# Weight copies from doubled loads, a split rounding step, the last odd skip on VectorE, and a new instruction order

## The chip, the cores and the metric

The kernel runs on one core of one Trainium2 chip. The metric is the device time of one execution in microseconds. A run of the profiler gives one execution in detail, with a time of its own. All times below are microseconds unless marked otherwise.

## The reference

Two independent branches read two inputs of 2048 positions by 448 features, and their results stand side by side in the output.

```python
# branch A: 16 heads of 28, each position looks at itself and 7 earlier ones, 2 apart
qkv = x @ wqkv                              # 448 -> 3 * 448
idx = pos[:, None] - arange(8)[None] * 2    # masked where negative
logits = einsum("bhsd,bhswd->bhsw", q, kg) * 28 ** -0.5
o = einsum("bhsw,bhswd->bhsd", softmax(logits), vg) @ wo
# branch B: a diagonal complex recurrence over 2048 steps
Bu = einsum("bld,pd->blp", x, B_bar)        # B_bar from Lambda, dt, B
h = Lam_bar * h + Bu[:, t]                  # for every t
y = 2 * einsum("blp,dp->bld", hseq, C).real + x * Dskip
```

Tensors are bf16 in memory.

## The kernel before

**Layout.** Positions are paired: even and odd positions become two "parities", so that the window with step 2 is contiguous within a parity. `xA` and `xB` hold the two inputs transposed, 7 chunks of 128 rows by 1024 position pairs. Since 448 is three and a half times 128, the fourth chunk holds 64 rows of each parity, and matmuls over 448 features run as pairs of half-height (64-row) matmuls, one for each parity, side by side in the array. Each pair writes its own half of a two-bank PSUM unit; there are four such units (pool `mm`, function `unit`). A weight therefore must lie in both halves of the partitions. A pair's 14 matmuls are split into a part of 8 (node name with a trailing underscore) and a part of 6; between the two a one-element GpSimd memset, a "tick", keeps the halves in order (`pair`, `relay`, `halves`).

**Branch A.** Nodes v0 to v7 compute V for 128 pairs each, nodes q{1 or 0}{s}{c} compute K (1) or Q (0) for head group s and column chunk c (256, 256 and 512 columns); ev and eq nodes copy the results out of PSUM, on ScalarE or VectorE. V's weights `Wv` are loaded once, and VectorE copies them to the other partition halves (vw0 to vw2). The first two blocks of `xA` come as rows and are transposed on TensorE (xt0, xt1, copied out by xe00 to xe11); the other six come through transposing DMAs. The weights of Q and K are loaded once into `Wraw`, four chunks high, and copied into `Wpad`, in which each head's 28 columns are padded to 32 and both halves are filled. That copy is the node wp{q}{z} (`n_wp`, for Q or K and for half z of the heads): five instructions, since rows move across partition halves. Attention goes over 9 blocks: node s{parity}{b} computes a block's scores with quarter-height (32-row) matmuls, first a mask (line 740), then the heads (line 744); x nodes take the exponential on ScalarE; a{b} multiplies by V with full-height matmuls of 29 columns; n{b} normalizes on VectorE; ot{b} transposes the result by a DMA; vi{b} builds the shifted window of V by DMAs. Nodes w0 to w7 multiply by `wo` and we nodes copy the result out.

**Branch B.** Small vectors are loaded into `rows` and turned by node tr; pA, pB, e1, e2, p2, p3a and p3b work out constants. A table of sines and cosines over 512 steps is made by t0 (ScalarE), tk and ts (VectorE), t2 (sine), t3 (a sign bit cleared, 2048 elements a partition) and t4 (cosine). l1 and l2 scale the B matrices, wtx transposes them by DMA into `WT`; b{half}{k} multiplies x by them (98 512-column matmuls in all, line 804), be evacuates; ma, ri, sc, mb and ro turn, scan and turn back on VectorE, 7 state chunks in two halves of 512 steps. ctn and ctl load and transpose C, cg and ch nodes form two scaled copies `C1` and `C2`; g0 and g1 form a product for the even positions. y{t} gives the even rows of an output block and z{t} the odd rows. The odd rows also need x times Dskip: for blocks 0 to 3 by four small diagonal matmuls in z{t}, for blocks 4, 5 and 6 (`YD`) on VectorE, which forms the products ahead (xd{t}) and adds them while it copies z{t} out (ye{t}1). Block 7 is cut into columns 0 to 319 (z70, ye71) and 320 to 447 (z71, ye72), with its diagonal matmuls, so that the last store is small.

**Order.** The program is a list of nodes, each with costs for the engines that may run it, what it depends on, a rank, and for some an earliest time (`at`). Class `Plan` simulates the engines with those numbers, takes the ready node of the lowest rank whenever an engine is free, and so fixes the order in each engine's queue; the queues then run in that order and wait only for data. A rank is a line in an index for each kind of node (`RANK`). A change of tile shape on TensorE is priced by `TURN`, 0.1 us. Loads are written first, in a fixed order, most of them on SP's queue; each load that is issued by SP or ScalarE uses one of eight semaphores in turn, so an issue also waits until the load eight before it has landed. Two of the small vectors go by GpSimd's own queue.

Of the kernel before, what the change touches and what calls it, by code (L numbers as in the profile page):

```python
# [7 lines left out]
BF16 = mybir.dt.bfloat16  # L8
F32 = mybir.dt.float32
I32 = mybir.dt.int32  # L10
# [16 lines left out]
RANK = {"vi": (-544.75, 131.055), "v": (-110.39, 34.569), "q0": (63.48, 25.419), "q1": (-1326.93, 228.142), "s": (-380.99, 73.488), "a": (-188.15, 159.093),  # L27
        "b0": (56.3, -31.172), "b1": (2986.12, -242.123), "d0": (94.79, 241.448), "d1": (1628.45, -108.947), "l": (2486.1, 164.979), "t": (251.37, -53.356),
        "tk": (731.53, 100.376), "xd": (2178.91, -29.053), "cg": (593.37, 8.672), "ch": (1143.63, -50.034), "g": (436.44, 143.698), "y": (468.94, 183.089),
        "w": (1186.02, 1.256), "gu": (1304.36, -293.628), "q2": (430.19, -21.545), "wp": (-27.3, 132.469)}  # L30


class Plan:


    WAKE, TURN = 0.13, 0.1
# [180 lines left out]
def kernel(  # L217
# [34 lines left out]
    Wraw = t_([128, 4, 2 * D], BF16, "Wraw", "rC")  # L252
    Wpad = t_([128, 7, 2, 512], BF16, "Wpad", "rW")
    natW = t_([128, 7, 2 * D], BF16, "natW")
    Pt = t_([128, D], BF16, "Pt")
    Ctn = t_([112, 4, 256], BF16, "Ctn", "rF")
# [27 lines left out]
    wload = lambda q: (A_wqkv[0:384, D * q:D * q + D].rearrange("(k p) n -> p k n", p=128), A_wqkv[384:448, D * q:D * q + D])  # L284
# [5 lines left out]
    ACT.dma_start(Wv[0:64, 3, :], A_wqkv[384:448, 2 * D:3 * D])  # L290
# [7 lines left out]
    SP.dma_start(Wraw[0:64, 3, :], A_wqkv[384:448, 0:2 * D])  # L298
    SP.dma_start(Wraw[:, 0:3, D:2 * D], wmain(1))
    xbar_x(xA, xA2, 512, 640)  # L300
    SP.dma_start(Wraw[:, 0:3, 0:D], wmain(0))
# [8 lines left out]
    xbar_x(xB, xB2, 0, 256)  # L310
    xbar_x(xB, xB2, 256, 512)
# [16 lines left out]
    def g_pad(e):  # L328
        G.memset(Wpad[:, :, :, :].rearrange("p k q (h c) -> p (k q h) c", c=32)[:, :, 28:32], 0.0)
# [30 lines left out]
    def g_ct(e, i):  # L360
        SP.dma_start(Ctn[:, :, 64 * i:64 * i + 64], (ct_r, ct_i, ct_i, ct_r)[i])
# [21 lines left out]
    p = {}  # L383
# [69 lines left out]
    def n_t3(e):  # L453
        V.tensor_scalar(ang.bitcast(I32), ang.bitcast(I32), 0x7FFFFFFF, None, ALU.bitwise_and)
# [56 lines left out]
    def n_wp(e, q, z):  # L511
        o = Wpad[:, :, q, 256 * z:256 * z + 256].rearrange("p k (h c) -> p k h c", c=32)[:, :, :, 0:DH]
        i = Wraw[:, :, D * q + 224 * z:D * q + 224 * z + 224].rearrange("p k (h c) -> p k h c", c=DH)
        f = V.tensor_copy if e == "V" else ACT.copy
        f(o[:, 0:3], i[:, 0:3])
        f(o[0:64, 3], i[0:64, 3])
        f(o[64:128, 3], i[0:64, 0])
        f(o[0:64, 4:7], i[64:128, 0:3])
        f(o[64:128, 4:7], i[0:64, 1:4])
# [42 lines left out]
    def node(name, cost, fn, deps, rank, **kw):  # L562
        r = rank
        if isinstance(rank, tuple):
            g, i, off = rank if len(rank) == 3 else rank + (0,)
            r = RANK[g][0] + RANK[g][1] * i + off
        urgent = any(a["alloc"] == "mm" for a, j in kw.get("frees", ()))
        d = plan.add(name, cost, fn, deps, r * 0.01 - 100 if urgent else r, **kw)
        d["key"] = (rank, urgent)
        return d  # L570
# [15 lines left out]
    for i, f in enumerate(gms):  # L586
        gm.append(node(f"gm{i}", {"G": 0.45}, f, gm[-1:], 4))
# [3 lines left out]
    g_c = [node(f"ctn{i}", {"S": 0.6}, lambda e, i=i: g_ct(e, i), [], 5, lat=2.5) for i in range(4)]  # L591
# [23 lines left out]
    t3 = node("t3", {"V": 1.2}, n_t3, [t2], ("t", 0))  # L615
# [5 lines left out]
    for i in range(3):  # L621
        vw.append(node(f"vw{i}", {"V": (0.48, 0.18, 0.44)[i]}, lambda e, i=i: n_vw(e, i), vw[-1:], (-400, -399, -397)[i], at=(4.5, 5.3, 5.3)[i]))
    xr = []
    for i in range(2):
        h = {}
        x = node(f"xt{i}", {"P": 0.6}, lambda e, i=i, h=h: n_xt(e, i, h), [g_e], -500, alloc="mm", at=(4.3, 5.0)[i])
        xr.append([node(f"xe{i}{z}", {"A": (0.49, 0.37)[z], "V": (0.6, 0.47)[z]}, lambda e, i=i, z=z, h=h: n_xe(e, i, z, h), [x], -398,
                        frees=[(x, 0)]) for z in range(2)])
    wp = {(q, z): node(f"wp{q}{z}", {"V": 1.55, "A": 2.9}, lambda e, q=q, z=z: n_wp(e, q, z), [g_p], ("wp", 2 * z + 1 - q), at=9.7 if q else 11.8)
          for z in range(2) for q in (1, 0)}  # L630

# [17 lines left out]
    for i, m in enumerate(MS):  # L649
        h = {}  # L650
        l1 = node(f"l1{m}", {"A": 0.58, "V": 0.46}, lambda e, m=m, h=h: n_l1(e, m, h), [p2], ("l", i), alloc="wt", at=20.5)
        l2 = node(f"l2{m}", {"V": 0.70}, lambda e, m=m, h=h: n_l2(e, m, h), [l1], ("l", i), frees=[(l1, 0)])
        wtx[m] = node(f"wtx{m}", {"S": 1.32}, lambda e, m=m: SP.dma_start_transpose(WT[:, :, 128 * m:128 * m + 128], natW[:, m, :]),
                      [l2], 6, lat=2.1)
    xb1 = node("xb1", {"S": 4.1}, lambda e: xbar_x(xB, xB2, 512, 1024), [wtx[3]], 7, lat=2.0)

    def n_ct(e):
        SP.dma_start_transpose(CT[:, 0:3, :], B_C_re[:, 0:384])
        SP.dma_start_transpose(CT[:, 4:7, :], B_C_im[:, 0:384])
        for k in range(4):  # L660
            SP.dma_start_transpose(CT[:, 3:8:4, 112 * k:112 * k + 112], Ctn[:, k, :])
# [12 lines left out]
    def at_x(t):  # L674
        return (0, 0, 7.6, 8.5, 10.4, 12.4, 13.6, 14.8)[(t - 1) // 128]
# [27 lines left out]
    for c, (t0_, t1_) in enumerate(CH):  # L703
        for s in range(4):
            for q in (1, 0):
                h = {}

                def pe(part, q=q, s=s, t0=t0_, t1=t1_, h=h):
                    if part == 0:
                        h["ps"] = unit()  # L710
                    pair(h, part, h["ps"], t1 - t0, lambda o, k: Wpad[o:o + 64, k, q, 128 * s:128 * s + 128], lambda o, k: xA[o:o + 64, k, t0:t1])

                def ev(e, q=q, s=s, t0=t0_, t1=t1_, h=h):
                    evac(e, (Qt if q == 0 else Kt)[:, s, :, t0:t1], h["ps"][:, :, 0:t1 - t0])
                r = (f"q{c}", 2 * s + 1 - q)
                n0, n1 = halves(f"q{q}{s}{c}", 0.2157 * (t1_ - t0_) / 512, pe, [wp[q, s // 2]] + (xr[0] + xr[1] if c == 0 else []), r, h, at_x(t1_))
                qn[q, s, c] = node(f"eq{q}{s}{c}", ab(2 * (t1_ - t0_)), ev, [n1], r, frees=[(n0, 0)])
# [76 lines left out]
    for hf in range(2):  # L794
        for k in range(4):
# [40 lines left out]
            def ro(e, k=k, hf=hf, h=h, big=big):  # L836
# [7 lines left out]
                else:  # L844
                    V.tensor_tensor(hb[0:64, 3, to], a[0:64, 0, 0], a[64:128, 0, 1], ALU.subtract)
                    V.tensor_tensor(hb[64:128, 3, to], a[64:128, 0, 0], a[0:64, 0, 1], ALU.add)
                    if hf == 0:
# [3 lines left out]
                      rb_, alloc="mm", at=24.8)  # L851
# [90 lines left out]
    YD = (4, 5, 6)  # L942
# [3 lines left out]
    def n_xn(e):  # L946
        xo = sk["x"] = t_([128, 4, D], BF16, "xo", "Kt")
        SP.dma_start(xo[:, 0:3, :], B_x[0].rearrange("(b t two) d -> t b two d", two=2, t=128)[:, YD[0]:YD[2] + 1, 1, :])
        SP.dma_start(xo[:, 3, :], B_Dskip.partition_broadcast(128))
    xl = node("xn", {"S": 1.2}, n_xn, sdone, 25, lat=3.0)  # L950

    def n_xd(e, i):
        if i == 0:
            sk["d"] = t_([128, 3, D], F32, "xd", "Qt")
        V.tensor_tensor(sk["d"][:, i, :], sk["x"][:, i, :], sk["x"][:, 3, :], ALU.mult)
# [29 lines left out]
    for t in range(8):  # L985
# [24 lines left out]
        def piece(e, lo, n, ds, tk=tk, h=h):  # L1010
            ps, hb = unit(), hbuf(1)
            h["z", lo] = ps
            for m in range(7):
                PE.matmul(ps[:, 1, 0:n], hb[:, m, 385:513], lazy["C1"][:, m, lo:lo + n], start=(m == 0), stop=False, skip_group_check=True)  # L1014
            for k in ds:
                a, b = (0, 64) if k == 0 else (128 * k - 64, 128 * k + 64)
                PE.matmul(ps[:, 1, a - lo:b - lo], xB[:, 3 + k, tk], dgO[:, k, 0:b - a], start=False, stop=(k == ds[-1]), skip_group_check=True)
# [16 lines left out]
        elif t in YD:  # L1034
# [5 lines left out]
        else:  # L1040
            n2 = node(f"ye{t}0", ab(D), lambda e, ev=ev: ev(e, 0, 1), [n0] + qdone, r, frees=[(n0, 0)])
            node(f"yo{t}0", {"S": 0.6}, lambda e, st=st: st(e, 0, 1), [n2], 60 + 3 * t, lat=2.2)
            for i, (lo, n, ds) in enumerate(((0, 320, (0, 1, 2)), (320, 128, (3,)))):
                n0 = n1 = node(f"z{t}{i}", {"P": (1.15, 0.52)[i]}, lambda e, lo=lo, n=n, ds=ds, piece=piece: piece(e, lo, n, ds),
                               [n0] + c1, (r[0], r[1], -0.1), alloc="mm")
                n3 = node(f"ye{t}{1 + i}", {"VA"[i]: (0.42, 0.2)[i]}, lambda e, lo=lo, n=n, h=h: evac(e, h["o"][:, 1, lo:lo + n], h["z", lo][:, 1, 0:n]),
                          [n1, n2], r, frees=[(n1, 0)])
                node(f"yo{t}{1 + i}", {"S": 0.5}, lambda e, lo=lo, n=n, tk=tk, h=h: SP.dma_start(outv[tk, 1, D + lo:D + lo + n], h["o"][:, 1, lo:lo + n]),
                     [n3], 61 + i + 3 * t, lat=2.2)
# [6 lines left out]
    plan.run({"P": 4.3, "A": 4.5, "V": 1.0, "S": 23.2, "G": 2.7})  # L1056
# [34 lines left out]
```

## Time and profile before

| | |
|---|---|
| median of 11 runs | 134.22 (133.88 to 134.7) |
| the profiled execution | 134.36 |
| its span, first to last instruction | 132.65 |
| TensorE busy, share of the span | 126.0, 95% |
| VectorE busy | 107.6, 81% |
| ScalarE busy | 90.2, 68% |
| GpSimd busy | 27.3, 21% |
| mean granted TensorE clock | 0.996 |
| DMA | 17.26 MB, mean 130 GB/s |

In the profile PE is TensorE, PEld its weight loads, DVE VectorE, ACT ScalarE, POOL GpSimd, SP the engine that issues most DMAs. The slices cut the span into 40 equal parts of 3.3 us, and a digit is the busy share in tenths. A waits line gives the total, the number and the longest wait. In the timeline and in the chain of work the first number is the start, the second the duration; brackets hold the idle time before it and what ended it. "issue" is time for which the profile shows no releaser.

### The profile page before, as it was taken

How to read it: one execution, taken by the hardware profiler on the slowest of the kernel's cores; microseconds unless marked ns; L12 is line 12 of the kernel's file. 1: busy time of each engine (PE TensorE's matmuls, PEld its weight loads, DVE VectorE, ACT ScalarE, POOL GpSimd, SP SyncE). 2: the span in 40 equal slices, each digit the busy share in tenths (PEclk: the TensorE clock that was granted, in tenths of full speed). 3: DMA queues.
4: the chain of work that ended last, by engine and by line, in shares of the span. 5: the costliest groups of instructions: out<-in, count | busy, mean ns of one | idle time of the engine just before them, and what ended most of it. 6: DMA issues, size and time to landing. Idle time of an engine off the chain costs nothing.

```text
span 132.7 us, 3798 instructions
## 1 busy us (share of the span) xinstructions
PE 126.0 (95%) x1528; PEld 70.7 (53%) x1533; DVE 107.6 (81%) x193; ACT 90.2 (68%) x121; POOL 27.3 (21%) x108
## 2 busy tenths in 40 slices
PE   6999999999999899999999999999999999999980
PEld 2555766786445445446454554655675655455550
DVE  0439999899879999999999999999999899921130
ACT  0729899989998946989999899724775266211120
POOL 6965146210899600000000000000000000000000
PEclk9999999999999999999999999999999999999998
DMA  3999979509949999451504114388345657442231
GB/s 98 326 242 222 260 165 218 90 8 101 181 79 155 165 195 130 103 125 27 132 5 105 28 50 87 95 232 124 102 105 152 164 89 269 146 138 74 69 104 45
DMA packets 42432, 17.26 MB, mean 130 GB/s; under 512 B 33452, under 2 KB 42412, under 8 KB 42412
## 3 DMA queue, kind: packets, MB, share of 16 engines
q1 hardware_dynamic: 41840, 16.58, 58.3%
q10 hardware_dynamic: 508, 0.40, 1.0%
q8 instruction: 13, 0.21, 0.7%
q14 instruction: 7, 0.06, 0.2%
q0 software_dynamic: 64, 0.00, 0.0%
HBM read 4.08 MB, written 3.67 MB: 58 GB/s over the span
## 4 chain that ended last, share of the span: by engine, by line
PE 82%; DVE 8%; ACT 4%; issue 2%; POOL 0%; POOLq 0%; ACTq 0%
PE mm L546 27%; PE mm L804 13%; PE mm L996 8%; PE mm L1003 7%; PE mm L763 5%; PE mm L998 5%; PE mm L895 4%; PE mm L740 3%; PE mm L547 3%; PE mm L1055 2%; PE mm L744 2%; DVE rs L833 1%; PE mm L1014 1%; DVE ra L815 1%; ACT wtmp L529 1%
## 5 line engine op out<-in xcount | busy, mean ns | idle before, releaser
L750 ACT ACTIVATE P<-mm 128x896 bf16<-128x896 f32 (+1 forms) x36 | 31.5, 929 | 2.1 <-PE mm L744 1.9
L546 PE MATMUL mm<-xA,Wpad 64*128 64x256 bf16 (+1 forms) x168 | 27.2, 305 | 0.4 <-POOL tick L554 0.4
L547 PE MATMUL mm<-xA,Wpad 64*128 64x256 bf16 (+1 forms) x168 | 27.2, 306 | 0.1
L523 ACT CAST ys<-mm 128x896 bf16<-128x896 f32 (+2 forms) x15 | 11.3, 764 | 23.1 <-PE mm L1003 8.9
L804 PE MATMUL mm<-xB,WT 128*128 128x512 bf16 x93 | 22.2, 379 | 0.6 <-DVE O L770 0.3
L554 POOL MEMSET tick<- 1x1 f32 x40 | 4.8, 120 | 84.2 <-PE mm L547 84.1
L546 PEld LDWEIGHTS <-Wpad 64*128 64x128 bf16 x168 | 14.9, 94 | 8.9 <-POOL tick L554 1.4
L547 PEld LDWEIGHTS <-Wpad 64*128 64x128 bf16 x168 | 14.7, 94 | 1.2 <-issue 0.5
L804 PEld LDWEIGHTS <-WT 128*128 128x128 bf16 x98 | 9.1, 97 | 10.9 <-issue 0.8
L547 PE MATMUL mm<-Wv,xA 64*128 64x448 bf16 x56 | 12.4, 350 | 0.3 <-DVE xA L525 0.2
L546 PE MATMUL mm<-Wv,xA 64*128 64x448 bf16 x56 | 12.7, 351 | 0.0
L996 PE MATMUL mm<-C,h 128*128 128x448 bf16 x56 | 11.9, 353 | 0.0
L546 PE MATMUL mm<-wo,OT 64*128 64x448 bf16 x56 | 10.8, 350 | 0.0
L547 PE MATMUL mm<-wo,OT 64*128 64x448 bf16 x56 | 10.8, 349 | 0.0
L1003 PE MATMUL mm<-C,h 128*128 128x448 bf16 x49 | 10.4, 353 | 0.0
L770 DVE TENSOR_TENSOR O<-mm,rcs 112x896 bf16<-112x896 f32 (+1 forms) x9 | 9.8, 1092 | 0.3
L523 ACT CAST u<-mm 128x1024 bf16<-128x1024 f32 (+1 forms) x8 | 7.2, 903 | 3.4 <-PE mm L804 3.4
L833 DVE TENSOR_TENSOR_SCAN rs<-p_r,ini,rv 128x512 bf16<-128x512 f32 x7 | 8.7, 1272 | 0.0
L833 DVE TENSOR_TENSOR_SCAN rs<-p_r,rv 128x512 bf16<-128x512 f32 x7 | 8.4, 1229 | 0.0
L763 PEld LDWEIGHTS <-P 128*128 128x128 bf16 x288 | 7.9, 96 | 1.0 <-issue 0.4
L1036 DVE TENSOR_TENSOR ys<-mm,xd 128x448 bf16<-128x448 f32 x3 | 1.9, 625 | 8.0 <-ACT ys L523 8.0
L815 DVE TENSOR_TENSOR ra<-u,tab 128x2048 bf16<-128x2048 bf16 x6 | 7.4, 1228 | 0.7 <-DVE h L841 0.5
(178 smaller groups left out, 242.0 us busy)
## 6 DMA issues: line engine op xcount, KB each, us to landing
out_dram<-ys SPq DMA_DIRECT2D x15, 224.0 KB, 2.4
Wraw<-in_A_wqkv_dram SPq DMA_DIRECT2D x2, 336.0 KB, 3.9
wo<-in_A_wo_dram SPq DMA_DIRECT2D x2, 336.0 KB, 3.2
P<-in_A_x_dram SPq DMA_DIRECT2D x2, 224.0 KB, 3.4
vw<-Va SPq DMA_DIRECT2D x2, 203.0 KB, 3.9
vw<-Va SPq DMA_DIRECT2D x2, 174.0 KB, 4.1
Wv<-in_A_wqkv_dram ACTq DMA_DIRECT2D x1, 336.0 KB, 3.7
natW<-in_B_B_re_dram SPq DMA_DIRECT2D x1, 336.0 KB, 4.2
```

Source lines behind the costliest of these rows:

```text
L523: ACT.copy(o, i)
L546: x = PE.matmul(ps[:, a, 0:n], lhs(0, lo[i]), rhs(0, lo[i]), start=(i == 0), stop=(i == 6), skip_group_check=True)
L547: y = PE.matmul(ps[:, b, 0:n], lhs(64, hi[i]), rhs(64, hi[i]), start=(i == 0), stop=(i == 6), skip_group_check=True)
L750: ACT.activation(P[:].rearrange("p s g q -> p g s q")[:, 2 * z:2 * z + 2, :, 0:n], h["s"][z][:, :, 0:4 * n].rearrange("p g (s q) -> p g s ...
L763: PE.matmul(av[:, par, 29 * hd:29 * hd + 29], hb_[par]["P"][:, hd // 4, hd % 4, :], v[:, par, hd, :], start=True, stop=True)
L770: V.tensor_tensor(O[0:n, :].rearrange("p (a h d) -> p a h d", a=2, h=H), avv[0:n, :, :, 0:DH], rc.unsqueeze(3).to_broadcast((n, 2, H, DH)) ...
L804: PE.matmul(ps[:, i, :], WT[:, j, 128 * m:128 * m + 128], xB[:, j, HALF * hf:HALF * hf + HALF], start=(j == 0), stop=(j == 6))
L815: V.tensor_tensor(a[:], x[:].unsqueeze(1).to_broadcast((128, 2, 2, HALF)), tab[:, :, k, :].unsqueeze(2).to_broadcast((128, 2, 2, HALF)), A ...
L833: V.tensor_tensor_scan(h["s"][:, i], p["r2"][:, k:k + 1].to_broadcast((128, HALF)), h["v"][:, i], 0.0 if hf == 0 else ini[:, m:m + 1], ALU ...
L996: PE.matmul(ps[:, 0, 0:D], hb[:, m, lo:lo + 128], lazy["C2"][:, m, :], start=(m == 0), stop=False, skip_group_check=True)
L998: PE.matmul(ps[:, 0, 0:D], xB[:, k, tk], Gm[:, k, :], start=False, stop=(k == 3), skip_group_check=True)
L1003: PE.matmul(ps[:, 1, 0:D], hb[:, m, lo + 1:lo + 129], lazy["C1"][:, m, :], start=(m == 0), stop=(t in YD and m == 6), skip_group_check=True)
```

## The change

- `Wraw` becomes two tiles, `Wr[1]` for K and `Wr[0]` for Q, each seven chunks high. Each is filled by four DMAs (`w_load`), which read the weights twice, so that all seven chunks stand in their final partitions. `n_wp` is then one instruction. `Wpad` is renamed `Wp`.
- The 64-row piece of `Wv` is issued by GpSimd, ahead of its two vector loads, instead of by ScalarE.
- The first half of `xB` comes in four transposing DMAs instead of two, the second half in three instead of one. `Ctn` shares memory with Q's weights, so its four loads wait for the copies wp00 and wp01 and stand between the transposes of `WT`.
- `n_t3` is four instructions of 512 elements a partition.
- Block 7 joins `YD`: its skip product is formed on VectorE, z70 and z71 lose their diagonal matmuls, ye71 and ye72 are additions on VectorE, and the last store is issued by ScalarE instead of SP.
- `RANK` has new numbers, a table `FINE` shifts single nodes, several costs and earliest times are new, and the planner's starting clocks too. The order of all queues changes with them.

Orders on TensorE from the first scores to the last V product, before and after:

```
before  q032_ q031 q132_ q032 s00 q132 b00 s10 b01 s01 a0 b03 s11 b02 s02 a1 q022_ q122_ q022 q122 s12 q012_ q112_ q012 q112
        s03 q002_ q102_ q002 q102 a2 s13 b13 s04 b12 s14 a3 b11 s05 g0 s15 a4 g1 s06 b10 s16 a5 y0 z0 s07 y1 z1 s17 a6 y2 s08
        z2 a7 s18 y3 z3 a8 w0_ w1_ w0 w1 w2_ w3_ ...
after   q122 q120_ q031_ q032_ q120 q031 q032 s00 b00 s10 b01 s01 a0 q132_ q022_ q132 s11 q022 b03 s02 a1 b02 s03 q012_ q112_
        q012 q112 s12 q002_ q102_ q002 q102 b13 a2 s13 b12 s04 a3 g1 s14 g0 s05 a4 b11 s15 b10 s06 a5 y0 s16 z0 y1 s07 z1 a6
        s17 y2 z2 s08 w0_ w1_ w0 w1 s18 a7 y3 a8 z3 w3_ w2_ ...
```

The queues of the other engines move with it: be00, eq022, eq002, ev5 and wp00 go from ScalarE to VectorE, xe01, ge1, wp11, ev4, eq112, eq120 and eq132 the other way; gu1 stands behind ro10 instead of ahead of it, we2 ahead of it.

```diff
+    def w_load(q):
+        w = A_wqkv[:, D * q:D * q + D]
+        SP.dma_start(Wr[q][:, 0:3, :], w[0:384].rearrange("(k p) n -> p k n", p=128))
+        SP.dma_start(Wr[q][0:64, 3, :], w[384:448])
+        SP.dma_start(Wr[q][64:128, 3, :], w[0:64])
+        SP.dma_start(Wr[q][:, 4:7, :], w[64:448].rearrange("(k p) n -> p k n", p=128))
...
-    ACT.dma_start(Wv[0:64, 3, :], A_wqkv[384:448, 2 * D:3 * D])
+    G.dma_start(Wv[0:64, 3, :], A_wqkv[384:448, 2 * D:3 * D])
...
-    SP.dma_start(Wraw[0:64, 3, :], A_wqkv[384:448, 0:2 * D])
-    SP.dma_start(Wraw[:, 0:3, D:2 * D], wmain(1))
+    w_load(1)
     xbar_x(xA, xA2, 512, 640)
-    SP.dma_start(Wraw[:, 0:3, 0:D], wmain(0))
+    w_load(0)
...
-    xbar_x(xB, xB2, 0, 256)
-    xbar_x(xB, xB2, 256, 512)
+    xbar_x(xB, xB2, 0, 128)
+    xbar_x(xB, xB2, 128, 256)
+    xbar_x(xB, xB2, 256, 384)
+    xbar_x(xB, xB2, 384, 512)
...
     def n_t3(e):
-        V.tensor_scalar(ang.bitcast(I32), ang.bitcast(I32), 0x7FFFFFFF, None, ALU.bitwise_and)
+        for k in range(4):
+            V.tensor_scalar(ang[:, k].bitcast(I32), ang[:, k].bitcast(I32), 0x7FFFFFFF, None, ALU.bitwise_and)
...
     def n_wp(e, q, z):
-        f(o[:, 0:3], i[:, 0:3])
-        f(o[0:64, 3], i[0:64, 3])
-        f(o[64:128, 3], i[0:64, 0])
-        f(o[0:64, 4:7], i[64:128, 0:3])
-        f(o[64:128, 4:7], i[0:64, 1:4])
+        (V.tensor_copy if e == "V" else ACT.copy)(
+            Wp[:, :, q, 256 * z:256 * z + 256].rearrange("p k (h c) -> p k h c", c=32)[:, :, :, 0:DH],
+            Wr[q][:, :, 224 * z:224 * z + 224].rearrange("p k (h c) -> p k h c", c=DH))
...
+            if name in FINE:
+                rank = rank[:2] + ((rank[2] if len(rank) == 3 else 0) + FINE[name],)
...
+        g_c.append(node(f"ctn{i}", {"S": 0.6}, lambda e, i=i: g_ct(e, i), g_c[-1:] + [wp[0, 0], wp[0, 1]], 5, lat=2.5))
...
-    YD = (4, 5, 6)
+    YD = (4, 5, 6, 7)
...
             for m in range(7):
-                PE.matmul(ps[:, 1, 0:n], hb[:, m, 385:513], lazy["C1"][:, m, lo:lo + n], start=(m == 0), stop=False, skip_group_check=True)
-            for k in ds:
-                a, b = (0, 64) if k == 0 else (128 * k - 64, 128 * k + 64)
-                PE.matmul(ps[:, 1, a - lo:b - lo], xB[:, 3 + k, tk], dgO[:, k, 0:b - a], start=False, stop=(k == ds[-1]), skip_group_check=True)
+                PE.matmul(ps[:, 1, 0:n], hb[:, m, 385:513], lazy["C1"][:, m, lo:lo + n], start=(m == 0), stop=(m == 6), skip_group_check=True)
...
+                    V.tensor_tensor(h["o"][:, 1, lo:lo + n], h["z", lo][:, 1, 0:n], sk["d"][:, 3, lo:lo + n], ALU.add)
...
+                    (ACT if e == "A" else SP).dma_start(outv[tk, 1, D + lo:D + lo + n], h["o"][:, 1, lo:lo + n])
```

## The prediction

> **What bounds the kernel now.** I read the page's busy shares and slices first, then the waits, then the timeline at the places that the change touches. The profiled execution took 134.36 us, 0.14 above the median of the runs (134.22); its span is 132.65 and 1.71 lies around it.
>
> ```profile
> PE 126.0 (95%) x1528; PEld 70.7 (53%) x1533; DVE 107.6 (81%) x193; ACT 90.2 (68%) x121; POOL 27.3 (21%) x108
> PE   6999999999999899999999999999999999999980
> DVE  0439999899879999999999999999999899921130
> ACT  0729899989998946989999899724775266211120
> PEclk9999999999999999999999999999999999999998
> ```
>
> TensorE is busy in every slice from 3 to 131 us at the full clock. So an edit pays only if it takes work or a stall off TensorE's queue, or shortens the first 5 or the last 4 us; VectorE is full from 10 to 113 us and can become the limit.
>
> ```profile
> PEld L740 <- issue: 4.8, 12, 0.4
> PEld L547 <- DVE Wpad L519: 0.5, 1, 0.5
> PE mm L804 <- DVE O L770: 0.3, 1, 0.3
> 22.44 0.43 issue
> 22.86 0.38 POOL tick L554
> ```
>
> From the waits (first three) and the chain (last two): TensorE stalls 0.5 us for a weight copy at 12.6, some 0.6 near 23 for a GpSimd tick, 0.3 for VectorE before b02 at 45.7. The large item is "issue" before L740, the mask matmul that opens each score block: 12 times 0.4.
>
> ```profile
> 38.28 0.10 PEld L740 LDWEIGHTS <-msk 32*128 32x128 bf16 x4 [0.42 <-issue]
> 99.13 0.10 PEld L740 LDWEIGHTS <-msk 32*128 32x128 bf16 x4
> ```
>
> Timeline of weight loads: s10 follows b00 (512-column matmuls) and starts 0.42 late; s18 follows a7 (29-column matmuls) and starts at once. The gap is the last matmul running out before the tile shape changes.
>
> ```profile
> 32.92 2.01 ACT L457 ACTIVATE tab<-tmpB,p_hpi 128x2048 bf16<-128x2048 f32 x1
> 34.96 1.28 ACT L750 ACT_TABLE_LOAD   x1
> 36.25 1.94 ACT L750 ACTIVATE P<-mm 128x1024 bf16<-128x1024 f32 x2
> ```
>
> ScalarE at the start of attention: t4, the table load, then the two exponentials of s00, without a gap. Their end (38.2) frees the PSUM unit that b01 needs (38.83 on TensorE).
>
> ```profile
> 128.43 0.49 DVE L525 CAST ys<-mm 128x320 bf16<-128x320 f32 x1 [1.94 <-PE mm L1017]
> 128.88 0.27 ACT L523 CAST ys<-mm 128x128 bf16<-128x128 f32 x1 [0.96 <-PE mm L1017]
> 128.95 0.82 SPq L1048 DMA_DIRECT2D out_dram<-ys  x2
> ```
>
> The end: both last stores go one after the other on SP's queue, done at 129.77; SP then reads the flag (129.82), waits out its semaphores and ends at 132.65.
>
> **Weight copies.** A copy is one instruction, not five. ScalarE: 0.75 us for 672 elements a row, 0.38 for 224, so 0.84 ns an element plus 0.19; 1568 elements come to 1.5 us against 3.0 (0.75+0.38+0.38+0.75+0.75). VectorE: 0.39 and 0.19, so 0.8 us, up to 2.1 if it meets a GpSimd memset as the 0.95 us copy at 19.2 did; I take 1.0 against 1.9 and 2.1. This frees 3 us of ScalarE and 2 of VectorE between 10 and 21 us. None is on TensorE, but the 0.5 stall before q121 and late evictions go.
>
> **Their loads.** K and Q come as four DMAs each, 784 KB for 392: eight issues for three on SP, 0.6 us each, +3.0 us for all behind them. In bytes: by 9.5 us 1975 KB had landed since 2.0 (264 KB/us), so 784 KB more also means 3 us. What waits, with the landings of before moved: x columns 512 to 640 from 9.5 to about 10.8, v4 needs them at 11.3; K weights about 10, the copy starts at 10.3 when ScalarE is through with ev0; Q 14, wanted at 16.5; the last x chunk 14.5 to 17.7, wanted after 22; B matrices 19.5 to 22.7, where l10 stands at 22.3 on ScalarE; xB's first half 23.4 to 26.6, b00 wants it at 34. The four xB loads cost two more issues, 2.5 us of SP for 3.8 before becoming 5.0; each also waits for the landing eight issues back. vi1, the four Ctn loads and the WT transposes queue behind them: the first transpose can issue at about 26 (29.15 before, when VectorE was late with l20), lands in 3.1 to 4.5, and b00 wants it by 34. All hidden, with 0.5 us to spare at v4 and l10 and more elsewhere. Without that cover v4 would pay one for one.
>
> **The last V rows by GpSimd.** It issues Wv's 64-row piece ahead of its two vector loads; those took 0.78 and 0.53 and landed 4.5 and 4.2 us after issue (0.9 KB). Behind it on GpSimd stand both vector loads, then eye (2.63), which the first transposes want at 4.29: one more issue of 0.5 to 1.0 ends it by 4.2. VectorE's vw1 waits for the piece, behind it vw2 and xe11, behind xe11 v1's matmuls. On ScalarE's queue it landed at 5.6; 1.32 plus 4.5 gives 5.8. vw1 then starts at 5.9 (6.28 before, behind xe01, which moves to ScalarE) and xe11 ends at 7.1, not 7.45. Bounds: 5.3 (gain 0.3 more) to 8.0 (2.2 lost); I take 5.8, the nearest row. A rule of the Trainium skill speaks against it (SBUF — State Buffer, the "DVE blocks DMA" trap): GpSimd writes such descriptors itself and is locked out while VectorE runs a fast two-port copy. The rows: the memset at 0.94 ends at 1.27 and vw0 starts at 4.48, and GpSimd's issues lie between. By the rows nothing is lost; by the rule, if the issue ran into vw0's 0.83 us, xe11 would end at 7.9 and the sum be 0.5 worse. I take the rows.
>
> **Up to b01.** Laying the new queue end to end with the old durations (v half 0.76 and 0.57, 256-column q half 0.44 and 0.33, plus 0.1 per tick), I reach q020 at 21.3; the same work was done at 22.0 before. The 23 us tick stall has no counterpart, as the memsets that held GpSimd then stand ahead of other ticks. s00 comes at about 33.2 with one half projection more done: 1.2 ahead. But ScalarE must evict q120 and q031 (TensorE done about 31.8 and 32.2), then t4 2.0, table 1.28, two exponentials 1.94: 32.9 to 38.1. b01 waits for that: 38.2 against 38.83. So **-0.6**; the other 0.6 is lost there. Bounds -1.2 (evictions earlier) and +0.9 (start late).
>
> **Rounding in four parts.** 512 f32 elements took 0.47 (the tk rows), 2048 took 1.21: with overlap four take about 1.6, +0.4. It ends at 32.2, and t4 waits for ScalarE until 32.9. Cover gone, +0.4 on the ScalarE chain above.
>
> **The order from b01 to y4.** Work per block is the same; the splices differ. Old and new both change tile shape 41 times after q032. The Trainium skill (TensorEngine Tiling (Array Packing), Key Properties) says that changing the tiling mode drains TensorE, with no size; at equal price per change the order costs nothing. The rows price a change by what went before: 0.42 after a 512-column matmul, 0.37 after y or w (448), 0.24 after g0, 0.10 or less after z0 to z3 and a. After b01 both have ten exits at 0.42, but the old leaves y or w twice (y2, w7), the new four times (y0, y1, w1, w7): **+0.74**. The planner's own price is a flat 0.1, so it did not see this. The stall before b02 (**-0.32**) has no counterpart, as b03 and b02 no longer wait for n0. Other waits over the four PSUM units come out positive but thin: s02 wants eq022 (48.4 against 48.8), q102 eq112, s13 eq102, b12 be13 (0.3 to spare), y0 the last C2 piece (82.9 against 83.4). Any may miss: **+0.2**, 0 to 1.2. VectorE from 39 us does one eviction and one scaling more, one Gm eviction less (+0.4), but be00 is now its own, so ma00 starts at 38.5, not 39.67; gu1 leaves the chain, we2 enters. ro10 ends near 113, y4 starts at 114.8. SP's later loads (vi, wo, xo and its fourth block) keep over 1 us.
>
> **The last odd skip.** Four diagonal matmuls leave z70 and z71; z0 with its four takes 1.69, z4 without 1.23, so 0.46 of TensorE. VectorE gets xd7 (0.62, at 113 to 115, before ye41 at 118) and ye72 (0.3, after ye71). From z70's first load at time t: old flag at t+2.2 but SP free at t+2.87; new ye71 t+1.35 to 1.82, ye72 to 2.1, flag t+2.25, and SP, with one store fewer, reads it at t+2.3. ScalarE's store, issued t+2.15, lands 1.5 later (the old row), t+3.65, as SP gets to its semaphore. So **-0.57**, bounds -0.8 and -0.2.
>
> **Sum.** -0.6 + 0.74 - 0.32 + 0.2 - 0.57 = -0.55. On the profiled 134.36 this is 133.8; on the median, **133.7 us**.
>
> **Rivals.** (a) Slower: the GpSimd piece lands late. Past 5.8 every us delays v1_ and all that follows; 0.6 is ScalarE's slack at b01, the 0.55 goes next, so it decides from about 7.0. At 8.0 the time is 134.22 - 0.55 + 2.2 - 0.6 = 135.3; at 7.4, 134.7. Against it: small loads on this queue landed at 5.8 and 6.3. (b) Near or above before: the tightly laid PSUM hand-overs miss by several tenths each, +1.2 for 0.2, giving 134.7; for it, VectorE and ScalarE are full from 39 to 83 us; against, most margins come out positive. (c) More than forecast: ScalarE reaches t4 earlier and b01 comes at 37.6, 133.0. (d) The copies and loads were hidden and the order neutral, so that only the tail's gain meets the drains: 134.22 + 0.74 - 0.57 - 0.32 = 134.1, no change that shows.
>
> **How the numbers follow.** Forecast 0.44 (133.1 to 134.0), (c) 0.14, (d) 0.10, (b) 0.18, (a) 0.14. Leaving out the far ends of (c) and (a) gives 132.7 to 135.0. A change under 0.2% (0.27 us) can't be told from none. Faster: forecast and (c), 0.58. Same: (d), 0.10. Slower: (a) and (b), 0.32.
>
> **What would show it.** Wp's copies at 1.5 and about 1 us; xe11 ending by 7.2; the last x chunk landing near 17.7; no tick wait near 23; b01 at 38.2 right after x001; "issue" before L740 at 0.37 behind y0, y1 and w1; last stores 129.0 or earlier, one from ScalarE. It is wrong if v1_ waits past 7.6, if TensorE stalls over 0.5 between 39 and 113, or if y4 waits for ro10.

## The result and the profile after

| | before | after |
|---|---|---|
| median | 134.27 (133.69 to 134.85, 52 runs) | 133.74 (133.48 to 134.23, 14 runs) |
| profiled execution, its span | 134.36, 132.65 | 134.00, 132.18 |

The ratio is 0.9962, with a 95% interval of 0.9952 to 0.9973: faster by 0.5 us, where 133.7 was forecast. The sum was right. Three of its four stretches were not, and their errors cancel. The profiled execution lies 0.26 above its median; its trace is used stretch by stretch.

The page of the changed kernel, busy shares and slices:

```profile
PE 125.4 (95%) x1523; PEld 71.9 (54%) x1529; DVE 107.2 (81%) x187; ACT 87.0 (66%) x115; POOL 27.8 (21%) x109
PE   5999998999979999999999999999999999999980
DVE  0517999999869799999999999999999999941140
ACT  3419998897995695799998948774849334511110
PEclk9999999999999999999999999999999999999999
```

Nothing has changed in kind. TensorE is still busy in every slice up to the last, at the full clock; its work is 0.6 us less (z70 and z71 have lost their diagonal matmuls), ScalarE's 3.2 us. So the difference must lie in stalls on TensorE's queue and at the ends. Its waits:

```profile
PE mm L584 <- DVE Va L563: 0.5, 1, 0.5
PE mm L782 <- ACT P L792: 0.4, 1, 0.4
PE mm L846 <- ACT P L792: 0.3, 1, 0.3
```

The stalls named before the change (q121's second part, the tick near 23, the one before b02) are gone. In their place stand one at 21.3 (q020's first part waits for ev5 to free a PSUM unit) and two between 37 and 39.1: s10 waits for the first exponential of s00, b01 for the second. The chain on ScalarE that leads there, in the timeline:

```profile
32.83 0.59 ACT L561 CAST Kt<-mm 128x512 bf16<-128x512 f32 x1 [0.93 <-PE mm L585]
33.31 0.59 ACT L561 CAST Qt<-mm 128x512 bf16<-128x512 f32 x1
33.79 2.02 ACT L500 ACTIVATE tab<-tmpB,p_hpi 128x2048 bf16<-128x2048 f32 x1
35.82 1.28 ACT L792 ACT_TABLE_LOAD   x1
37.12 2.85 ACT L792 ACTIVATE P<-mm 128x1024 bf16<-128x1024 f32 x3
```

ScalarE stands idle for 0.93 until TensorE has finished q120, then makes two copies (eq120, eq031) and only then t4, which had its input since 32.56. t4 ran at 32.92 before. The end of the program:

```profile
128.53 0.35 SPq L1087 DMA_DIRECT2D out_dram<-ys  x1
128.62 0.14 DVE L976 TENSOR_SCALAR flag<-mm 1x1 int32<-1x1 f32 x1
128.73 0.38 ACTq L1087 DMA_DIRECT2D out_dram<-ys  x1
```

The two last stores are issued by two engines, 0.2 apart, and SP is free for the flag at 128.93 (129.82 before).

Some nodes on TensorE divide the span into stretches: b01 by its first matmul, y4 and z70 by their first weight load. For b01 the load will not do as a mark. In the changed kernel it runs ahead, at 38.74, and its matmul waits until x001 has ended at 39.05; before, load and matmul came together (38.83 and 38.84). Before, then after:

```profile
38.84 1.47 PE L804 MATMUL mm<-xB,WT 128*128 128x512 bf16 x6
39.11 1.24 PE L846 MATMUL mm<-xB,WT 128*128 128x512 bf16 x5 [0.30 <-ACT P L792]
```

| stretch | before | after | difference | forecast |
|---|---|---|---|---|
| start to b01 | 38.84 | 39.11 | +0.27 | -0.6 |
| b01 to y4 | 76.00 | 75.45 | -0.55 | +0.62 |
| y4 to z70 | 12.12 | 12.12 | 0 | 0 |
| z70 to the end | 5.70 | 5.51 | -0.19 | -0.57 |
| span | 132.65 | 132.18 | -0.47 | -0.55 |

The first row is not an unlucky execution. In the five kernels below that have the same queues up to b01 and the same loads, or differ from it only in Wv's piece, its first matmul comes at 39.09 to 39.94. So the change does not bring b01 forward in any trace; what it gains, it gains behind b01 and at the end.

### The profile page after: what moved, and what is told of

The parts are those of the page before. It is cut to its first block, busy times and chain, and to the rows that moved or that the text cites. A ratio compares the mean times of both kernels' runs of the same rounds, so it can differ in the third digit from the quotient of the medians.

```text
span 132.2 us, 3796 instructions
## 1 busy us (share of the span) xinstructions
PE 125.4 (95%) x1523; PEld 71.9 (54%) x1529; DVE 107.2 (81%) x187; ACT 87.0 (66%) x115; POOL 27.8 (21%) x109
## 4 chain that ended last, share of the span: by engine, by line
PE 84%; DVE 4%; ACT 4%; DMA 3%; issue 2%; SPq 0%
PE mm L584 30%; PE mm L846 14%; PE mm L1038 8%; PE mm L1045 7%; PE mm L805 6%; PE mm L1040 5%; PE mm L937 4%; PE mm L782 4%; DMA P<-in_A_x_dram 3%; PE mm L786 2%; PE mm L585 2%; ACT P L792 1%; DVE Wp L555 1%; DVE Kt L563 1%; ACT L792 1%
## 5 line engine op out<-in xcount | busy, mean ns | idle before, releaser
L584 PE MATMUL mm<-xA,Wp 64*128 64x256 bf16 (+1 forms) x168 | 26.5, 305 | 0.5 <-DVE Va L563 0.5
L585 PE MATMUL mm<-xA,Wp 64*128 64x256 bf16 (+1 forms) x168 | 26.5, 305 | 0.0
L561 ACT CAST ys<-mm 128x896 bf16<-128x896 f32 (+1 forms) x14 | 11.0, 801 | 19.5 <-PE mm L1045 8.9
L592 POOL MEMSET tick<- 1x1 f32 x40 | 4.3, 108 | 83.1 <-PE mm L585 82.9
L584 PEld LDWEIGHTS <-Wp 64*128 64x128 bf16 x168 | 15.4, 94 | 6.3 <-POOL tick L592 0.3
L585 PEld LDWEIGHTS <-Wp 64*128 64x128 bf16 x168 | 15.2, 94 | 1.0 <-issue 0.8
L561 ACT CAST u<-mm 128x1024 bf16<-128x1024 f32 (+1 forms) x7 | 6.2, 890 | 6.0 <-PE mm L846 6.0
L584 PEld LDWEIGHTS <-OT 64*128 64x128 bf16 x56 | 5.1, 94 | 5.0
```

Of the source, the lines that this page charges most:

```text
L561: ACT.copy(o, i)
L584: x = PE.matmul(ps[:, a, 0:n], lhs(0, lo[i]), rhs(0, lo[i]), start=(i == 0), stop=(i == 6), skip_group_check=True)
L585: y = PE.matmul(ps[:, b, 0:n], lhs(64, hi[i]), rhs(64, hi[i]), start=(i == 0), stop=(i == 6), skip_group_check=True)
```

## The experiments

In all of them the order of every queue is written out, so that nothing moves but what the edit names. Medians that were not taken side by side differ by a few tenths of a microsecond where the traces show less, so a small effect is read from the stretches of the trace. Ratios are to the kernel before, with their 95% intervals.

**One part alone: the tail.** The old order and loads, with the new last odd skip:

```diff
-    YD = (4, 5, 6)
+    YD = (4, 5, 6, 7)
...
-                PE.matmul(ps[:, 1, a - lo:b - lo], xB[:, 3 + k, tk], dgO[:, k, 0:b - a], start=False, stop=(k == ds[-1]), skip_group_check=True)
+                    V.tensor_tensor(h["o"][:, 1, lo:lo + n], h["z", lo][:, 1, 0:n], sk["d"][:, 3, lo:lo + n], ALU.add)
```

> The kernel before with its own order, and of the change only the last odd skip: xd7 stands on VectorE behind xd5, z70 and z71 lose their diagonal matmuls, ye71 and ye72 are additions on VectorE, ScalarE issues the last store. The forecast's step says -0.57 us (-0.8 to -0.2), so a ratio of 0.996: the flag is written and read 0.5 earlier and nothing else is late. The rival, from the trace of the changed kernel: SP reads the flag 0.6 earlier, but its first instruction behind the branch comes 0.5 after it instead of 0.2, so only 0.2 to 0.3 us (0.998) comes through.

Measured: 134.04 against 134.32, ratio 0.9977 (0.9952 to 1.0002). From z70 to the end the trace has 5.19 us against 5.70, so -0.51: the forecast's -0.57, not the rival's 0.2 to 0.3. (The medians differ by 0.28 only, with an interval that reaches 1; the stretch is the sharper measure, as it is 5.50 or 5.51 in nine of the traces made from the changed kernel, that one included.) SP's first instruction behind the branch comes 0.15 after it, as before. In the changed kernel it comes 0.47 after it, and in every kernel made from the changed one it is 0.47 too, whatever was edited, but for two: 0.71 in wv_act, and 0.15 in best2, where 0.43 appears between two later instructions of SP. The next experiment has 0.47 as well.

**One part alone: loads and copies.** The old order with the doubled loads, the one-instruction copies and the split xB loads:

```diff
-    SP.dma_start(Wraw[0:64, 3, :], A_wqkv[384:448, 0:2 * D])
-    SP.dma_start(Wraw[:, 0:3, D:2 * D], wmain(1))
+    w_load(1)
     xbar_x(xA, xA2, 512, 640)
-    SP.dma_start(Wraw[:, 0:3, 0:D], wmain(0))
+    w_load(0)
```

> The kernel before with its own order, and of the change only the doubled loads of the K and Q weights with copies of one instruction, the xB loads in more parts and the memory that goes with them (Wv's 64-row piece stays on ScalarE's queue). The forecast's reading: the stall of 0.5 before q121's second part goes, ScalarE is 3 us and VectorE 2 us freer between 10 and 21 us, all later landings are hidden, so b01 comes about 0.5 us earlier and so does the end: 0.996. A rival: loads that land 3 us later meet this order, which was not laid for them, at v4, the B matrices and the WT transposes: b01 no earlier, or later by up to 0.5: 1.000 to 1.004.

Measured: 134.55, ratio 1.0020 (0.9998 to 1.0042); b01 at 38.70, like the 38.74 of tail_only. The rival was right. The timeline of weight loads, at q121's second part, and the waits of this kernel:

```profile
13.03 0.09 PEld L577 LDWEIGHTS <-Wp 64*128 64x128 bf16 x1 [0.55 <-POOL tick L585]
```

```profile
PE mm L796 <- DMA vw<-Va: 0.8, 1, 0.8
PE mm L577 <- DMA xA<-in_A_x_dram: 0.4, 1, 0.4
PE mm L577 <- POOL tick L585: 0.3, 1, 0.3
```

The copy takes 0.63 on VectorE, but TensorE waits the same 0.55: behind the copy stood a GpSimd tick. The later landings are not hidden either: TensorE waits 0.68 for x columns before v5_, and 1.3 before a2 for the window loads vi2, which SP issues at 57.83 (56.39 before), behind the CT transposes. Six of the 14 runs lie above 135.1 and the others below 134.7; the profiled one is of the upper group. So this part is worth nothing in the old order, and the waits it adds are real. Whether an order made for it uses what it frees was not run by itself; the changed kernel, which has such an order, is no earlier at b01 either.

**What sets b01: ScalarE's chain.** The changed kernel, with eq120 and eq031 moved to VectorE directly behind t3, and eq032, which VectorE had already, behind them:

```diff
-... V:t3 ... P:q031 V:l22 A:eq120 P:q032 A:eq031 S:ctn2 V:l26 P:s00 A:t4 S:wtx2 V:eq032 P:b00 ...
+... V:t3 ... P:q120 P:q031 V:eq120 V:eq031 P:q032 V:eq032 V:l22 S:ctn2 V:l26 P:s00 A:t4 S:wtx2 P:b00 ...
```

> The changed kernel with eq120, eq031 and eq032 on VectorE directly behind t3, ahead of l22 and l26, so that ScalarE goes from eq122 straight to t4. Theory: ScalarE's chain t4, table load, x000, x001 sets b01 (38.73); t4 then starts near 32.6 instead of 33.79, x001 ends near 37.9, and TensorE, which is then the limit, reaches b01 near 38.1. VectorE's 1.4 us more lie in its idle time before be00. So -0.6 us: 0.9955. The rival: TensorE itself, or the units that VectorE frees later, holds b01 where it is, or what is gained is waited for later by VectorE's chain of scans: 0 to -0.2 us, 0.9985 to 1.000.

Measured: 133.07, ratio 0.9914 (0.9892 to 0.9936), 0.7 us better than the changed kernel. Its ScalarE:

```profile
32.57 2.00 ACT L528 ACTIVATE tab<-tmpB,p_hpi 128x2048 bf16<-128x2048 f32 x1 [0.69 <-DVE tmpB L525]
34.59 1.28 ACT L820 ACT_TABLE_LOAD   x1
35.89 1.94 ACT L820 ACTIVATE P<-mm 128x1024 bf16<-128x1024 f32 x2
38.08 1.94 ACT L820 ACTIVATE P<-mm 128x1024 bf16<-128x1024 f32 x2 [0.26 <-PE mm L814]
```

t4 now waits for t3 alone, x001 ends at 37.83, and b01's first matmul comes at 37.92, 1.19 earlier, directly behind s10. The last line shows the roles changed: ScalarE waits for TensorE. VectorE ends l23 at 37.50 and starts be00 at 37.47 (37.48 in the changed kernel), so the two copies more do not delay its next chain. From b01 to y4 it takes 75.62, so 0.17 of the 1.19 is given back, and y4 comes 1.0 earlier.

**Exits from y and from z.** Two score blocks of the changed kernel stand behind z instead of behind y:

```diff
-P:y0 P:s16 P:z0 ... A:x160 ... A:x161 ... P:y1 A:ye0 ... P:s07 ... P:z1
+P:y0 P:z0 P:s16 ... A:ye0 A:x160 ... A:x161 ... P:y1 ... P:z1 ... P:s07
```

> The changed kernel with two score blocks moved: y0, z0, s16, y1, z1, s07 instead of y0, s16, z0, y1, s07, z1, and the copies ye0 and ye1 ahead of x160 and x070 on ScalarE. The number of shape changes is the same; two exits from y (gap 0.37 each) become exits from z (gap 0.10 or less). The forecast's pricing by gaps says -0.54 us: 0.996. A price that is equal for every change says 0: 1.000 within 0.001, with the z blocks that stand before a score block longer by what the gap loses.

Measured: 134.89, ratio 1.0050 (1.0032 to 1.0069), over 1 us worse than the changed kernel. Neither theory said so. The trace shows a wait of 0.6 at a6 for the window of block 6: the store yo0 had moved ahead of vi6 on SP. So it ran again with both stores left in place (the same edit, but yo0 and yo1 behind vi6 and vi7):

> y_exits again with the stores yo0 and yo1 left behind the window loads vi6 and vi7 on SP, where the changed kernel has them: in y_exits the window of block 6 came late and a6 waited 0.6 us for it. Theory by now: exits from y and from z cost the same, so the time of the changed kernel, ratio 0.996 to before, and no wait at a6. The pricing by gaps: -0.54 us more, 0.992.

Measured: 134.82, ratio 1.0009 (0.9969 to 1.0049). The timeline of weight loads of the changed kernel, and then of this one:

```profile
83.89 1.07 PEld L1038 LDWEIGHTS <-h 128*128 128x128 bf16 x7
...
86.08 0.10 PEld L782 LDWEIGHTS <-msk 32*128 32x128 bf16 x4 [0.37 <-issue]
...
86.58 1.06 PEld L1045 LDWEIGHTS <-h 128*128 128x128 bf16 x7
...
88.06 0.15 PEld L1038 LDWEIGHTS <-h 128*128 128x128 bf16 x2
```

```profile
84.72 1.06 PEld L1066 LDWEIGHTS <-h 128*128 128x128 bf16 x7
...
86.64 1.23 PEld L1073 LDWEIGHTS <-h 128*128 128x128 bf16 x7
...
88.44 0.10 PEld L810 LDWEIGHTS <-msk 32*128 32x128 bf16 x4
...
88.94 0.11 PEld L1066 LDWEIGHTS <-h 128*128 128x128 bf16 x2
```

From y0 to y1 the first has 4.17 us (with a gap of 0.37), the second 4.22 (without a gap). Where no score block stands between, z's first load runs ahead of y's last matmuls and z then takes longer: 1.80 from its first load to the score block, not 1.48. The gap is a load that can't run ahead, and the time of the block beside it is shorter by as much. Up to s17 both kernels take 9.33 us. The rest of the loss is a new wait: s07 comes later, so do its exponentials, and s17 and y2 wait for the units they free (0.48 within s17 and 0.3 at y2's first matmul).

The kernel before shows the same by itself, if one measures from first matmul to first matmul. Here y0, z0 and s07, then y2, s08, z2 and a7:

```profile
84.81 1.48 PE L996 MATMUL mm<-C,h 128*128 128x448 bf16 x7
...
86.89 1.49 PE L1003 MATMUL mm<-C,h 128*128 128x448 bf16 x7
...
88.50 0.37 PE L740 MATMUL mm<-msk 32*128 32x448 bf16 x4
```

```profile
94.03 1.49 PE L996 MATMUL mm<-C,h 128*128 128x448 bf16 x7
...
96.20 0.37 PE L740 MATMUL mm<-msk 32*128 32x448 bf16 x4
...
96.70 1.50 PE L1003 MATMUL mm<-C,h 128*128 128x448 bf16 x7
...
98.24 0.96 PE L763 MATMUL mm<-vw,P 128*128 128x29 bf16 x32
```

y takes 2.08 ahead of z and 2.17 ahead of a score block; z takes 1.54 ahead of a full-height block and 1.61 ahead of a score block. An exit costs 0.07 to 0.09 from either, although the gap is 0.37 behind y and 0.10 behind z.

**The price of a change of tile shape.** One matmul of 16 columns more between y and z of the blocks 4, 5 and 6, 32 rows high in one kernel and 128 in its twin:

```diff
+            if t in (4, 5, 6):
+                PE.matmul(ps[:, 1, 0:16], msk[0:32, 0, :], msk[0:32, 1, 0:16], start=True, stop=True, skip_group_check=True)
```

> The changed kernel with one extra matmul of 32 rows and 16 columns between y and z of the blocks 4, 5 and 6, in a stretch where TensorE sets the end; what it writes is overwritten by z's first matmul. Each visit adds an exit to quarter-height tiles and the way back, so six shape changes. The forecast's pricing by gaps: 0.37 out of y, 0.10 back, and the way of the matmul itself as in the full-height twin (visit128): about +1.4 us more than the twin. The rival, that a change drains TensorE at an equal price both ways (0.3 to 0.4 each, from the block durations): +1.8 to +2.4. If changes of shape cost nothing beside the matmul: 0.

> The twin of visit32: the same three extra matmuls of 16 columns, but 128 rows high, so that the tile shape never changes. Both theories: below +0.1 us each, +0.1 to +0.3 us against the changed kernel.

Measured: 134.97 and 134.17 (ratios 1.0029, 0.9999 to 1.0059, and 0.9958, 0.9916 to 1.0001). From y4 to z70 the trace has 12.78 and 12.20, against 12.12 without a visit. The first visit, weight loads, 32 rows and then 128:

```profile
117.13 0.09 PEld L1073 LDWEIGHTS <-msk 32*128 32x128 bf16 x1 [0.37 <-issue]
117.25 1.06 PEld L1075 LDWEIGHTS <-h 128*128 128x128 bf16 x7
118.40 0.29 PEld L1066 LDWEIGHTS <-h 128*128 128x128 bf16 x2
```

```profile
116.98 0.10 PEld L1073 LDWEIGHTS <-msk 128*128 128x128 bf16 x1
117.17 1.07 PEld L1075 LDWEIGHTS <-h 128*128 128x128 bf16 x7
118.33 0.29 PEld L1066 LDWEIGHTS <-h 128*128 128x128 bf16 x2
```

The full gap of 0.37 is there, yet the visit costs 0.19 more than its twin ((12.78 - 12.20) / 3), so about 0.1 for each of its two changes, if they cost the same; by the medians (0.80 in all) 0.13. Both theories had it too large.

**The memsets beside wp01.** v_evict, with six GpSimd memsets in later gaps:

```diff
-... G:one1 ... G:zer0 ... G:zer1 ... G:zer2 ... G:zer3 ... G:rcs ... G:v6k ... G:q130k ... G:v7k
+... G:v6k G:one1 G:zer0 G:zer1 ... G:q130k G:zer2 G:zer3 ... G:v7k G:rcs
```

> v_evict and, on GpSimd, the six long memsets that stood from 19 to 22 us (one1, zer0 to zer3, rcs) in later gaps between ticks. Theory: VectorE's copy wp01 took 1.63 us for 0.61 of wp00 because it shared its time with those memsets; freed, wp01 takes 0.6 to 0.8, ev5 ends near 20.8 instead of 21.74, TensorE's wait of 0.5 before q020's first part goes, and since TensorE sets b01 in v_evict, the end comes 0.5 us earlier: 0.9875 to before. The rival: the gain is lost to the tick, to ScalarE's evictions or to t4, as in the forecast's own case: 0.991 as v_evict.

Measured: 132.96, ratio 0.9854 (0.9798 to 0.9910; the runs of before that this was timed beside spread more than the others, and v_evict is 0.1 away by the medians, so a gain over v_evict is not shown). VectorE of the changed kernel, then of this one:

```profile
19.13 1.63 DVE L555 COPY Wp<-Wqr 128x1568 bf16<-128x1568 bf16 x1
20.68 1.07 DVE L563 CAST Va<-mm 128x896 bf16<-128x896 f32 x1
```

```profile
19.38 0.62 DVE L583 COPY Wp<-Wqr 128x1568 bf16<-128x1568 bf16 x1
20.21 1.09 DVE L591 CAST Va<-mm 128x896 bf16<-128x896 f32 x1 [0.22 <-PE mm L613]
```

The same copy takes 0.62 instead of 1.63 once the memsets are gone from beside it; TensorE's wait for ev5 is gone and b01 comes at 37.53 (37.92 in v_evict), though x columns came 0.36 later in this execution. Then 0.9 is lost again, at a2, and the waits name it:

```profile
PE mm L833 <- DMA vw<-Va: 0.9, 1, 0.9
```

It is vi2 behind the CT transposes once more (issued at 58.09). The last experiment gives that issue to ScalarE and also takes up the x columns.

**x columns earlier, and vi2 by ScalarE.** The changed kernel with one load moved, and `best` with this and vi2:

```diff
+    xbar_x(xA, xA2, 640, 768)
     w_load(0)
-    for i in range(5, 8):
+    for i in range(6, 8):
```

> The changed kernel with the transposing load of x columns 640 to 768 ahead of the four loads of Q's weights instead of behind them. Theory by now: the forecast's 'all hidden' holds only for an early landing; in several traces TensorE waits 0.3 to 0.7 us for x columns before v4_ or v5_, and b01 moves with it one for one. With this order v5_ never waits, v4_ may still: -0.1 to -0.4 us against the changed kernel in the median, ratio 0.993 to 0.996 to before. The rival: the same wait moves to Q's weights (wp00) or to v4_: no change, 0.996.

> best with two more edits: the load order of x5_first, and the window loads of block 2 (vi2) issued by ScalarE behind x031 instead of by SP behind the CT transposes. Theory: in best a2 waited 0.9 us for that window, which SP, busy without a pause from 22 to 59 us, could issue only at 58.1; issued at 53 it lands by 57, and the wait goes, so -0.5 to -0.9 us against best; with x5_first's share 0.980 to 0.983 to before. The rival: the wait only hid another one (ScalarE's exponentials or VectorE's scans), or ScalarE's issue costs as much: 0.985 as best.

Measured: x5_first 134.26, ratio 1.0019 (0.9987 to 1.0050): no gain. v4_ still waits (0.4), and Q's weights now land so late that wp00 starts at 17.78 (16.74 in v_evict); TensorE waits 0.2 at q001_ for wp00 itself and 0.3 at q000_ for a copy that stands behind it on VectorE. The rival was right. best2: 133.14, ratio 0.9921 (0.9897 to 0.9945), no better than v_evict or best. Half of it did what it was made for: ScalarE issues vi2 at 53.17, no wait for a window is left, and from b01 to y4 it takes 75.74 us against 76.50 in best. The moved load spends that gain, as q001_ waits for wp00, which starts at 18.10 (16.65 in best):

```profile
PE mm L613 <- DVE Wp L584: 0.4, 1, 0.4
```

b01 is at 38.03. best with vi2 on ScalarE and the x load left alone was not run.

**Two edits put back.** The rounding step as one instruction, and Wv's piece on ScalarE's queue:

```diff
-        for k in range(4):
-            V.tensor_scalar(ang[:, k].bitcast(I32), ang[:, k].bitcast(I32), 0x7FFFFFFF, None, ALU.bitwise_and)
+        V.tensor_scalar(ang.bitcast(I32), ang.bitcast(I32), 0x7FFFFFFF, None, ALU.bitwise_and)
```

> The changed kernel with the rounding step as one instruction of 2048 elements again. The forecast's step: four parts cost 0.4 us of VectorE and end by 32.2, hidden until ScalarE gets to t4, so one part saves 0.2 (four took 1.42, one 1.21 before) that nothing sees: no change, 0 within 0.15 us. The rival: the long instruction holds the GpSimd ticks behind q120 and q031 back until its end, near 32.3, and delays q120's second part by 0.2 to 0.5 us, which comes through as eq120 and eq031 stand on ScalarE's chain: +0.2 to +0.5.

Measured: 134.30, ratio 1.0028 (0.9996 to 1.0061). VectorE and GpSimd in this kernel:

```profile
31.34 1.22 DVE L524 TENSOR_SCALAR tmpB<-tmpB 128x2048 int32<-128x2048 int32 x1
```

```profile
31.50 1.39 POOL L619 MEMSET tick<- 1x1 f32 x3 [1.56 <-PE mm L612]
```

And GpSimd in the changed kernel, where t3 runs from 31.14 to 32.56 in four parts:

```profile
31.29 0.63 POOL L592 MEMSET tick<- 1x1 f32 x2 [1.56 <-PE mm L585]
32.59 0.09 POOL L592 MEMSET tick<- 1x1 f32 x1 [0.67 <-PE mm L585]
```

With one long instruction, three ticks that begin at 31.50 last to 32.89, past its end at 32.56; with four, the first two are through by 31.92. From q120's first part to its second it takes 2.09 instead of 1.74; less of this is left by b01, which comes 22.14 behind v5_ instead of 22.00, so 0.14 us in all. The rival's mechanism is there, at less than its size.

```diff
-    G.dma_start(Wv[0:64, 3, :], A_wqkv[384:448, 2 * D:3 * D])
+    ACT.dma_start(Wv[0:64, 3, :], A_wqkv[384:448, 2 * D:3 * D])
```

> The changed kernel with Wv's 64-row piece issued by ScalarE again. The forecast's step: the piece lands near 5.8 either way and v1's matmuls wait for xe11, not for vw1, so no change, 0 within 0.15 us, and GpSimd's own vector loads and the eye tile 0.8 us earlier. The rival by the rule that a queue run by GpSimd is held up by VectorE: vw1 and xe11 come earlier by up to 0.5 us with ScalarE's queue, -0.5.

Measured: 134.19, ratio 1.0008 (0.9981 to 1.0034). vw1 starts at 5.80 with ScalarE's queue and at 5.71 with GpSimd's, so the rival's half microsecond is not there. v1_ comes at 6.84, 0.1 to 0.6 earlier than in the traces with GpSimd's, but v4_ then waits for x columns, and v5_ (17.10) and b01 (39.09) stand where they were. The loss at the branch is 0.71 in this program.

## Why the prediction was right

**Copies: right.** 1.50 on ScalarE, 0.61 and 1.63 on VectorE (taken: 1.0; the first lies below the lower figure of 0.8).

**GpSimd's piece: right.** It landed at 5.68 (forecast 5.8) and vw1 started at 5.71. xe11 ended at 7.45, not 7.1, but it waited for ScalarE's copy xe10 (6.47 to 7.06, behind the transpose xt1), not for vw1, which the forecast's sum did not have. The lock-out that the Trainium skill (SBUF — State Buffer, the "DVE blocks DMA" trap) warns of was not put to the test at this place: GpSimd's issue ended at 2.11, and VectorE's first copy began at 4.58. GpSimd and VectorE did hold each other up at t3 and at wp01.

**Loads, "all hidden": wrong in part.** The spare 0.5 at v4 is not there. x columns 512 to 640 landed at 11.69, not 10.8, and the last x chunk at 18.37, not 17.7. In other executions of the same loads v4_ waited up to 1.1 us and v5_ up to 0.7; b01 moves one for one with v5_ (17.10 to 17.96 and 39.09 to 39.94, with ScalarE's chain unchanged). The window loads vi2, of which the forecast said that SP's later loads keep over 1 us, have no room either.

**Up to b01, -0.6: wrong, +0.27 measured.** The mechanism (b01 waits for ScalarE's chain q120, q031, t4, table, two exponentials) was right, and v_evict shows it; the term mis-sized is the chain's start. The forecast had TensorE done with q120 near 31.8, and eq120 could start only at 32.83; t4 started at 33.79 instead of 32.9, and x001 ended at 39.05 instead of 38.1. Half of this is the 0.47 that TensorE lost at q020_ behind the copy of 1.63: s00 came at 33.70 for 33.2, and best shows the part of the memsets. The other half is where q120 was laid: 1.4 ahead of s00 in the forecast, 0.87 in the trace.

**t3, +0.4 and hidden: its sign was missed.** It costs 0.20 of VectorE, which is hidden (t4 waits for ScalarE until 33.79), and by the traces it gives TensorE 0.14, through the ticks.

**Order from b01 to y4, +0.62: wrong, -0.55 measured.** The step that failed is the choice of the row prices for the exits, +0.74. The gap before a mask load is not a price: y_exits2 gives the same time with and without it up to s17, and a change of shape costs about 0.1, behind y as behind z. The rule of the Trainium skill that was weighed against the rows (TensorEngine Tiling (Array Packing), Key Properties: a change of mode drains), at an equal price per change, gives 0 and was the one to take; the planner's flat 0.1, which the forecast said did not see this, was the right size. The +0.2 for the small hand-overs was not there either: behind b01's first matmul the trace of the changed kernel shows no idle time of TensorE above 0.05. The gain is two stalls that went: from s11's first matmul to that of the next block 0.85 became 0.50 (the stall before b02, forecast -0.32), and from s13's 0.63 became 0.50 (not forecast: b13 starts at 62.45, just after ScalarE's copy eq102 has ended at 62.40). All other blocks together give -0.07.

**Tail, -0.57: right alone (-0.51), -0.19 in the whole.** The same 0.32 that SP loses behind the branch also appears with the loads alone (6.02 from z70 to the end, 5.70 before), so it comes with that part of the change and not with the tail. Why is open.

The errors are +0.87, -1.17 and +0.38, together +0.08. The forecast time was right since they cancelled, which is luck, not since its terms were.

## What to carry to other kernels

A gap with no releaser before a change of tile shape was not the price of the change here: a load that can't run ahead shortens the block beside it. So compare the times from first matmul to first matmul of the blocks on both sides of a move, or put in one visit and its twin; the first needs no new run, as the trace of before already had the answer. For the same reason take a stretch's border at a matmul and not at a weight load, which may run ahead of a wait. When a change frees an engine, look which chain stands at the next synchronisation and at what that chain waits for first: here two copies moved from the full chain to an engine that stood idle a little later gave more than the whole change. A load that is made longer to save a copy also moves everything behind it on its queue; look 30 us further down for what that queue issues late.

## What was not expected of the hardware

- A plain copy on VectorE of 1568 bf16 elements a partition took 0.62 us alone and 1.63 with GpSimd memsets beside it; a one-element GpSimd memset took 0.09 alone, and three of them ran to the end of a 1.22 us VectorE instruction that they met.
- A visit to another tile shape and back cost TensorE 0.19 us, so about 0.1 for a change, where the gap that one sees is 0.37.
- SP's first instruction behind the last branch came 0.15 or 0.47 us after it (0.71 once). Ten kernels with the new loads, of quite different times, all show 0.47, so it seems to belong to the program; with one trace of each this is not shown. It is 0.47 with both last stores on SP's queue (loads_only) and with one on ScalarE's. What decides it was not found.
